# Chunk 2's last output half a step later, the first-used half of v loaded first, one load of q moved, and the packing of an output reversed

## The chip, the cores and the metric

The kernel runs on one core of a Trainium2 chip. The metric is the device time of one execution in microseconds (us), median of several runs. A profile of one further execution shows when each engine worked: TensorE (PE for matmuls, PEld for the loads of their weights), VectorE (DVE), ScalarE (ACT), GpSimd (POOL) and SyncE (SP). SP, ACT and POOL each have a queue from which they issue transfers (DMA); sixteen DMA engines, shared by these queues, carry them out.

## What is computed

A gated recurrence over 768 tokens for 4 batches and 8 heads of 48 channels, followed by a gated MLP over all 3072 tokens:

```python
f = 1.0 / (1.0 + np.exp(-f_logit))                 # q, k, v, f_logit: (4, 8, 768, 48)
for t in range(S):
    state = f[:, :, t, :, None] * state + np.einsum('bhd,bhe->bhde', k[:, :, t], v[:, :, t])
    y[:, :, t] = np.einsum('bhd,bhde->bhe', q[:, :, t], state)
x = y.transpose(0, 2, 1, 3).reshape(B * S, H * D)  # (3072, 384)
g = x @ w_gate                                     # (384, 1536)
out = (g / (1.0 + np.exp(-g)) * (x @ w_val)) @ w_out
```

## The kernel before

**Units and chunks.** The tokens are cut into six chunks of 128, c = 0 to 5. One chunk of one batch is a unit (b, c); its number is u = 4c + b (`units`, L397). The recurrence of a unit (`attention`, L630) is a generator of fifteen steps: load and transpose f, k and q, running products of f, scores (L754), masks, the output y (L826 from the state, L837 from the chunk itself), the new state (dS, L808) and the packing of y into xT (`copy_y`, L841). In chunk 3, say, these run while TensorE works on the MLP of chunk 2: TensorE's own stream is the MLP, and the recurrence of the next chunk is put into it piece by piece.

**The MLP of a chunk** (`mlp_fifteen`, L1097, for chunks 1 to 5) first forms sums of its tokens on VectorE (`token_sums`, L1105), then runs four blocks of fifteen products (L1143, into the PSUM banks A, B, o and c) and then the way down (`down_seven`, L1223): seven products `one` to `seven` of 24 matmuls each (L1246, L1309), each in two half steps of twelve. xT has three rows of 128 features (row 0, 1, 2) for 512 tokens. The first of the token sums, t14, needs rows 1 and 2 for batches 0 and 1. The second, t15, needs row 2 for all batches, and the fourth (on 512 columns) needs all three rows for batches 2 and 3. The last product `seven` leaves its results (`ob`) to two VectorE sums that stand behind the token sums of the next chunk. One of their inputs, u5, lies in the room `c22`, which ScalarE's copy of the second product (`c<-B`, L1148) overwrites at the start of the next chunk; the fifth product goes into bank B and waits for that copy.

**The order.** Tables of times say where in the MLP's stream each step of a unit stands: `SCORES` (when the scores come), `CHAINS` (the steps before them) and, in `times` (L1012), the time of each output. They are in microseconds of a model of TensorE's stream; `down[n]` is the n-th half step of the way down. `in_turn_of_time` (L1317) writes the instructions down in that order, and `in_order` (L896) keeps each engine's instructions in it. The last output of each chunk 2 to 5, that of batch 3, stands at `down[9]`: before the second half of `four` (o5, whose second half works on the hidden sums `hs`).

**Loads.** From unit 5 on, f, k and q are loaded in four pieces of 96 KB each into one room per name (`load`, L486). As there is one room, the next unit's load is issued right behind the step that emptied the room: `load_after(u, "f")`, `load_after(u, "k")` and `load_after(u, "q")` (L675, L687 or L721, L734). kT is turned by way of DRAM: four transfers out (L718) and one back as `kt` (L771 or L779), which dS reads.

**The two halves of v.** The score matrix of a unit is cut in blocks of 64 keys. L837 needs v in its usual place and, for the blocks that lie in the other half of the partitions, a second copy of parts of v, which `load_other_v` (L453) brings in two transfers of 48 KB: n = 0 for heads 0 to 3, n = 1 for heads 4 to 7. L837's loop takes the first 64 keys of all heads first. There the heads with `a` = 2 or 3 (heads 4 to 7) read the second copy; heads 0 to 3 read it in the second round.

**Packing.** `copy_y` copies y to SBUF with two ScalarE copies (even heads, then odd heads) and moves it into xT by ten transfers (L852), a head at a time, 48 features each, cut where a row of xT ends. GpSimd issues them, apart from units of chunks 0 and 1 with b < 3, where SP does.

**Completion semaphores.** The transfers of the queues of SP and ACT share eight completion semaphores and take them in turn. A transfer whose semaphore still belongs to one in flight waits on its queue for that one to land. GpSimd's transfers share another eight.

Of the kernel before, what the change touches and what calls it, by code (L numbers as in the profile page):

```python
# [290 lines left out]
def short_path(ctx, tc, ident, least, judge, q, k, v, f_logit, moe_w_gate, moe_w_val, moe_w_out, out):  # L291
# [10 lines left out]
    B, H, S, D = q.shape  # L302
# [13 lines left out]
    SQUARES = 2  # L316
# [80 lines left out]
    units = [(b, c) for c in range(NCH) for b in range(B)]  # L397
# [35 lines left out]
    def in_halves(u):  # L433

        b, c = units[u]
        return c > 0

    def blocks_of_keys(t, top, a, keys):

        t = t[top * CH:(top + 1) * CH]
        if keys:
            return t[:, (2 + a % 2) * CH:(3 + a % 2) * CH]
        return t.rearrange("p (two c) -> p two c", two=2)[:, :, a % 2 * CH:(a % 2 + 1) * CH]

    def other_v(A):

        return A.rearrange("p r a t -> p (r a t)")[:, 12 * CH:].rearrange("p (h e) -> p h e", e=W)

    def load_other_v(A, u):  # L453
        b, c = units[u]
        for n in range(2):
            since = c * C + (1 - n) * CH
            queue = nc.gpsimd if c < SQUARES and b == B - 1 else nc.sync
            queue.dma_start(out=other_v(A)[n * CH:(n + 1) * CH, :, 0:D],
                            in_=v[b, n * HP:(n + 1) * HP, since:since + CH, :].rearrange("h t d -> t h d"))
# [10 lines left out]
    def split_squares(nm):  # L470
        return squares(nm).rearrange("t a (j i) e -> t a j i e", j=2)
# [5 lines left out]
    def parted(t):  # L477

        return t.rearrange("p (j a t i) -> p a j i t", j=2, a=HP, i=NI // 2)
# [4 lines left out]
    def load(u, what="fkqv"):  # L486
        b, c = units[u]
        rows = slice(c * C, (c + 1) * C)
        inputs = dict(f=f_logit, k=k, q=q, v=v)
        for nm in "fqkv" if c >= SQUARES else "fvkq" if by_squares(u) else "fkqv":  # L490
            src = inputs[nm]
            if nm not in what:
                continue
            if nm == "v":
                dst = v_of(u)
            elif not by_squares(u):
                dst = raw[nm][u % NRAW]
            else:
                since = len(traced)
                for n in range(4):  # L500
                    at = Q * (1 - n % 2)
                    (nc.sync if c >= SQUARES else nc.gpsimd).dma_start(
                        out=rooms[nm][Q * n:Q * (n + 1), at:at + HP * RUN].rearrange("t (a e) -> t a e", a=HP),
                        in_=src[b, n // 2::2, rows, :].rearrange("a (t i) d -> t a (i d)", i=NI))
                if c < SQUARES:
                    by_pool.extend(ins for ins in traced[since:] if ins.engine == mybir.EngineType.Pool)
                    keep_order(by_pool[-5:])
                continue
            queue = nc.gpsimd if nm == "v" and c < SQUARES and (by_squares(u) or u in (1, 2)) else nc.sync
            for heads in (slice(0, HP), slice(HP, H)) if u == 0 and nm == "f" else (slice(0, H),):  # L510
                queue.dma_start(out=dst[:, heads, 0:D], in_=src[b, heads, rows, :].rearrange("h t d -> t h d"))
# [118 lines left out]
    def attention(u):  # L630
        b, c = units[u]
# [51 lines left out]
        if in_squares:  # L683
            kp = qT.rearrange("p a t -> p (a t)")
            nc.vector.transpose(parted(kp), split_squares("k"))
            if not turned or u == SQUARES * B:
                load_after(u, "k")  # L687
        yield

        n = HP * N1  # L690
        owner["tail", rot] = owner["start"] = u
        owned(u, ("gate", rot))
        for part in parts:
            at = slice(part.start * N1, part.stop * N1)
# [36 lines left out]
        if in_squares:  # L731
            qp = tail[:, 0:HP * C]
            nc.vector.transpose(parted(qp), split_squares("q"))
            load_after(u, "qv" if c < SQUARES else "q")  # L734
        yield
        owned(u, ("gate", rot), ("tail", rot))
        if halves and c < SQUARES:
# [74 lines left out]
        if halves:  # L812

            y = [bank("y") for _ in range(2)]

            def place(a, par, part=slice(0, W)):
                return y[a // 2][W * (a % 2) + part.start:W * (a % 2) + part.stop, par * C:(par + 1) * C]  # L820

            def of_state(pars_of, parts, first):
                for part in parts:
                    for a in range(HP):
                        par = pars_of(a)
                        nc.tensor.matmul(place(a, par, part), lhsT=decayed[rows_of(par), a, part], rhs=qT[rows_of(par), a, :],  # L826
                                         start=first, stop=False, skip_group_check=True)

            of_state(lambda a: 1 - a // 2, [slice(0, Q), slice(Q, W)], True)
            if SQUARES <= c < NCH - 1:  # L830
                dS = new_state()
            of_state(lambda a: a // 2, [slice(0, W)], False)
            for keys in range(2):
                for par in range(2):
                    for a in (0, 2, 1, 3):
                        h, top = 2 * a + par, a // 2
                        nc.tensor.matmul(queries_of_keys(place(a, par, slice(0, W if keys == top else D)), keys), rhs=blocks_of_keys(flat[par], top, a, keys),  # L837
                                         lhsT=(v_[:, h, :] if keys == top else other_v(A)[:, h % HP, 0:D])[top * CH:(top + 1) * CH],
                                         start=False, stop=keys == 1, skip_group_check=True)

            def copy_y():  # L841
                yT = att.tile([128, 2, TB // 2], FP32, tag="x", name="yT")
                for par in range(2):
                    nc.scalar.copy(yT[:, par, :], y[par][:, 0:HP // 2 * C])  # L844
                for h in range(H):
                    a, par = h // 2, h % 2
                    f = h * D
                    while f < (h + 1) * D:
                        n = min((h + 1) * D, (f // 128 + 1) * 128) - f
                        r = W * (a % 2) + f - h * D  # L850
                        queue = nc.sync if c < SQUARES and b < B - 1 else nc.gpsimd
                        queue.dma_start(out=xT[c][f % 128:f % 128 + n, f // 128, b * C:(b + 1) * C],  # L852
                                        in_=yT[r:r + n, a // 2, par * C:(par + 1) * C])
                        f += n

        else:


            y = bank("y")
            met = set()  # L860

            def add(n, lhsT, rhs, last):
                nc.tensor.matmul(y[Q * (n % 4):Q * (n % 4) + Q, n // 4 * C:(n // 4 + 1) * C], lhsT=lhsT, rhs=rhs,
                                 start=n % 4 not in met, stop=last, skip_group_check=True)
                met.add(n % 4)

            per = 2 * D // Q
            flat = v_.rearrange("t h e -> t (h e)")
            for par in range(2):
                for n in range(DM // Q):  # L870
                    h = n // per * 2 + par
                    at = n * Q - h * D
                    if -Q < at < D:
                        add(n, flat[:, W * h + at:W * h + at + Q], A[:, par, h // 2, :], par == 1 or at + Q <= D)
            nc.scalar.copy(xT[c][:, :, b * C:(b + 1) * C], y[:, 0:DM].rearrange("p (a t) -> p a t", t=C))
# [3 lines left out]
        if halves:  # L879
            copy_y()  # L880
# [10 lines left out]
    def load_after(u, what):  # L891

        if u + 1 < len(units) and u + 1 != SQUARES * B:
            load(u + 1, what)
# [99 lines left out]
    def chain(k, q, qmul, turn=None, head=None):  # L994
# [5 lines left out]
    down = [NJ * TRIPLE + n * DOWN / 2 - 0.05 for n in range(14)]  # L1000
# [5 lines left out]
        (chain(2.6, 4.8, 8.6), chain(14.5, 21.7, 23.2, 21.2, 19.6), chain(30, 37, 43.6), chain(57.4, 56.6, 61)),  # L1006
        (chain(-12, -8.5, -5), chain(3.5, 6, 9), chain(16, 28, 33, 21.5, 23.5), chain(40.1, 53, 55, 44.5, 52)),
        *[(chain(-21.4, -13.2, -11.5), (-7.5, -6.3, 1.3, 2.2, 3.2, 5.5, 8, 10), chain(16, 28, 33, 21.5, 23.5), chain(40.1, 53, 55, 44.5, 52))] * (NCH - 4)))}
    LAST = down[9]
    APART = {1: (1, 3), 2: (1, 2), **{c: (2,) for c in range(3, NCH - 1)}, NCH - 1: range(1, NJ)}  # L1010

    def times(c):  # L1012
        at = [t for t, _ in SCORES[c]]
        outputs = [*at[1:], down[9] if c + 1 in SCORES and SCORES[c + 1][0][0] < -1 else LAST]
        sigmoid = [-14 if c == 3 else SCORES[c - 1][-1][0] - whole - 0.01 if c > 3 else 0, -1.5 if c == 3 else at[0] - 0.01, *[t - 0.01 for t in at[1:]]]
        masks = {"b": 2, "o": 0.9, "A": 1.5}
        return [[f, *steps, s + 0.02, s + masks[kind], s + 2.2, o, o + 0.01, o + 2.1]
                for f, steps, (s, kind), o in zip(sigmoid, CHAINS[c], SCORES[c], outputs)]
# [504 lines left out]
```

## Time and profile before

| | us |
|---|---|
| median of 3 runs | 593.06 (592.43 to 593.49) |
| profiled execution | 589.34 |
| its span, first to last instruction | 587.6 |
| chunk 1's products begin | 136.5 |
| chunk 2's products begin | 231.95 |
| chunk 3's products begin | 323.67 |
| chunk 4's products begin | 415.98 |

The granted TensorE clock is 1.00 throughout. Lines of the profile read so: start (or line), duration, engine, source line, operation, what is written <- what is read, shape, number of instructions merged in the row, and in brackets the idle time of the engine before it and what ended it. In the chain of work that ended last, each line has a start, a length and what the program was waiting for or doing. In the view of waits a line says which engine waited at which line for whom: total us, times, longest. Transfers that are issued by SP or ACT stand on their queues, SPq and ACTq. A span of several issues merged in one row runs from the first to the end of the last.

### The profile page before, as it was taken

Reading aid. Unit: us, or ns where it says so; the run is one execution under the profiler, and the core shown is the slowest. Engines: PE = TensorE matmul, PEld = TensorE weight load, DVE = VectorE, ACT = ScalarE, POOL = GpSimd, SP = SyncE. Lnnn points to the kernel's source line nnn. Section 1 sums busy time; section 2 is a strip of 40 time slices with the busy share of each in tenths; the row PEclk is TensorE's granted clock in tenths of the full one; section 3 lists DMA queues with packets and bytes.
Section 4 is the critical chain, followed back from the end, with each engine's and each line's share of the span. In section 5 each row is a group of like instructions: output and inputs, shape, how many; then the busy total and the mean of one; then the engine's idle time right before and its main releaser. Section 6 shows DMA issues by size and latency. Waiting matters only on the chain.

```text
span 587.6 us, 12443 instructions
## 1 busy us (share of the span) xinstructions
PE 573.3 (98%) x4641; PEld 472.9 (80%) x4641; DVE 468.5 (80%) x825; ACT 303.7 (52%) x589; POOL 144.1 (25%) x307
## 2 busy tenths in 40 slices
PE   7999999999999989999999999999999999999996
PEld 4744445567888978888999788899988899988996
DVE  8888998999989975998985978986878971766641
ACT  2587778006887412666740476732376820356600
POOL 5140444341142334031233030333030323000000
PEclk9999999999999999999999999999999999999999
DMA  9999696434669557453446433434341100100001
GB/s 180 279 283 285 190 249 147 88 103 131 130 151 144 117 126 180 125 107 79 101 108 153 114 89 73 104 93 120 112 115 28 35 17 16 58 2 2 0 1 57
DMA packets 122643, 65.97 MB, mean 112 GB/s; under 512 B 79616, under 2 KB 112992, under 8 KB 122576
## 3 DMA queue, kind: packets, MB, share of 16 engines
q1 hardware_dynamic: 108508, 48.62, 33.7%
q0 software_dynamic: 12784, 14.67, 10.9%
q10 hardware_dynamic: 1284, 1.84, 0.9%
q8 instruction: 37, 0.61, 0.4%
q14 instruction: 30, 0.25, 0.1%
HBM read 50.14 MB, written 8.65 MB: 100 GB/s over the span
## 4 chain that ended last, share of the span: by engine, by line
PE 85%; DMA 6%; DVE 3%; ACT 2%; issue 2%; SPq 1%; ACTq 0%; POOL 0%; DVEq 0%
PE A L1143 17%; PE o L1246 15%; PE B L1143 14%; PE c L1143 6%; PE o L950 5%; PE gate L927 5%; PE val L927 5%; PE o L1143 5%; PE o L1309 3%; DMA kt<-turn 2%; PE y L826 2%; PE y L837 2%; PE sc L754 2%; PE dS L808 2%; DMA fraw<-in_f_logit_dram 2%
## 5 line engine op out<-in xcount | busy, mean ns | idle before, releaser
L852 POOL DMA_DIRECT2D xT<-yT x170 | 84.8, 508 | 91.6 <-ACT yT L844 83.2
L1143 PE MATMUL A<-xs,w_both 128*128 128x256 f32 x240 | 61.8, 380 | 0.0
L1246 PE MATMUL o<-w_out,h 128*128 128x192 f32 x360 | 61.2, 326 | 0.0
L1246 PEld LDWEIGHTS o<-w_out,h 128*128 128x128 f32 x360 | 59.0, 190 | 0.4
L1148 ACT COPY aside<-A 128x512 f32<-128x512 f32 x60 | 35.1, 585 | 33.1 <-PE A L1143 33.1
L1148 ACT COPY c<-A 128x512 f32<-128x512 f32 x40 | 23.3, 583 | 54.9 <-PE A L1143 44.5
L1044 DVE TENSOR_TENSOR c<-c,aside 128x512 f32<-128x512 f32 x60 | 41.2, 686 | 12.6 <-ACT aside L1148 10.6
L1143 PEld LDWEIGHTS A<-xs,w_both 128*128 128x128 f32 x240 | 45.2, 190 | 6.3
L1095 DVE TENSOR_TENSOR h<-h,c 128x256 f32<-128x256 f32 x100 | 40.4, 412 | 6.1 <-ACT h L1159 5.7
L741 POOL MEMSET gates<- 128x4 f32 x24 | 3.7, 153 | 161.4 <-DVE qT L648 155.5
L1047 DVE TENSOR_TENSOR c<-c,aside 128x512 f32<-128x512 f32 x60 | 40.9, 682 | 2.6 <-ACT aside L1148 2.6
L844 ACT COPY yT<-y 128x256 f32<-128x256 f32 x40 | 12.8, 370 | 58.6 <-PE y L837 42.0
L1143 PE MATMUL B<-xT,extra 128*128 128x256 f32 x160 | 41.3, 380 | 0.9 <-ACT c L1148 0.9
L1246 PE MATMUL o<-ws,h 128*128 128x192 f32 x240 | 41.7, 328 | 0.0
L1159 ACT ACTIVATE h<-c 128x256 f32<-128x256 f32 x100 | 39.2, 416 | 4.8 <-DVE c L1044 3.5
L1143 PE MATMUL A<-xs,extra 128*128 128x256 f32 x160 | 41.3, 380 | 0.3 <-ACT c L1148 0.2
L1143 PE MATMUL B<-xs,w_both 128*128 128x256 f32 x160 | 41.3, 380 | 0.0
L1143 PE MATMUL c<-xT,w_both 128*128 128x256 f32 x160 | 41.1, 379 | 0.0
L1148 ACT COPY aside<-B 128x512 f32<-128x512 f32 x60 | 35.1, 585 | 9.6 <-PE B L1143 7.3
L1246 PEld LDWEIGHTS o<-ws,h 128*128 128x128 f32 x240 | 39.3, 190 | 0.5
L1047 DVE TENSOR_TENSOR c<-o,c 128x512 f32<-128x512 f32 x40 | 27.3, 683 | 10.0 <-ACT h L1159 5.8
L1143 PEld LDWEIGHTS B<-xT,extra 128*128 128x128 f32 x160 | 30.2, 190 | 5.7 <-ACT c L1148 1.6
(173 smaller groups left out, 1250.0 us busy)
## 6 DMA issues: line engine op xcount, KB each, us to landing
fsquares<-in_f_logit_dram SPq DMA_DIRECT2D x64, 96.0 KB, 2.8
qsquares<-in_q_dram SPq DMA_DIRECT2D x64, 96.0 KB, 2.5
ksquares<-in_k_dram SPq DMA_DIRECT2D x64, 96.0 KB, 2.4
w<-in_moe_w_gate_dram SPq DMA_DIRECT2D x6, 768.0 KB, 8.1
w<-in_moe_w_val_dram SPq DMA_DIRECT2D x6, 768.0 KB
w<-in_moe_w_out_dram SPq DMA_DIRECT2D x6, 768.0 KB, 4.7
v<-in_v_dram SPq DMA_DIRECT2D x19, 192.0 KB, 5.3
kt<-turn SPq DMA_DIRECT2D x11, 256.0 KB
```

The lines of the kernel that those rows point to most:

```text
L844: nc.scalar.copy(yT[:, par, :], y[par][:, 0:HP // 2 * C])
L852: queue.dma_start(out=xT[c][f % 128:f % 128 + n, f // 128, b * C:(b + 1) * C], in_=yT[r:r + n, a // 2, par * C:(par + 1) * C])
L927: nc.tensor.matmul(p, lhsT=w[:, j, i, :], rhs=xT[c][:, i, :], start=(i == 0), stop=(i == KT - 1))
L950: nc.tensor.matmul(p, lhsT=hidden_tile(h, n // 2)[:, n % 2 * 2 + b // 2, b % 2 * C:(b % 2 + 1) * C], rhs=w_out[:, j, :], start=(n == 0), s ...
L1044: nc.vector.tensor_tensor(dst, a, b, ALU.add)
L1047: nc.vector.tensor_tensor(dst, a, b, ALU.subtract)
L1095: lagging.append(lambda: f(*args))
L1143: nc.tensor.matmul(p[name][:, n, :], lhsT=weights_of[a][:, n, j, :], rhs=tokens[b], start=fresh and n == 0, stop=True, skip_group_check=True)
L1148: nc.scalar.copy(t, p[name])
L1159: nc.scalar.activation(dst, src[:, 0, :], AF.Silu)
L1246: nc.tensor.matmul(p[:, n, :], lhsT=lhsTs[j][:, n * C:(n + 1) * C], rhs=rhs[:, j, :], start=first and j == order[0] and n == 0, stop=j == ...
L1309: nc.tensor.matmul(p, lhsT=hidden_tile(h, j)[:, 2, n * C:(n + 1) * C], rhs=b22[:, j, :], start=j == order[0], stop=j == order[-1])
```

## The change

Four edits. The last output of chunk 2 is set to `down[10]`, behind the second half of `four`; those of later chunks stay at `down[9]`. `load_other_v` issues n = 1 before n = 0, for all units that use it. For the units b = 1 of chunks 4 and 5 (`behind`), the load of q is no longer issued behind the step that emptied its room (the transposition of q of unit (0, c)) but behind the unit's own transposition of k. `copy_y` sends the pieces of xT from head 7 to head 0.

```diff
+    def behind(u):
+
+        return u < len(units) and units[u][1] > SQUARES + 1 and units[u][0] == 1
...
     def load_other_v(A, u):
         b, c = units[u]
-        for n in range(2):
+        for n in (1, 0):
...
             kp = qT.rearrange("p a t -> p (a t)")
             nc.vector.transpose(parted(kp), split_squares("k"))
+            if behind(u):
+                load(u, "q")
             if not turned or u == SQUARES * B:
                 load_after(u, "k")
...
             qp = tail[:, 0:HP * C]
             nc.vector.transpose(parted(qp), split_squares("q"))
-            load_after(u, "qv" if c < SQUARES else "q")
+            if not behind(u + 1):
+                load_after(u, "qv" if c < SQUARES else "q")
...
-                for h in range(H):
+                for h in reversed(range(H)):
                     a, par = h // 2, h % 2
...
-    LAST = down[9]
...
-        outputs = [*at[1:], down[9] if c + 1 in SCORES and SCORES[c + 1][0][0] < -1 else LAST]
+        outputs = [*at[1:], down[9] if c > SQUARES else down[10]]
```

(`SQUARES` is 2; before, both branches of `outputs` gave `down[9]`.) On TensorE, this is chunk 2's last output (unit 11; y, dS) before the change, with the first half of `four` (on hs_1375) ahead of it. Line numbers are those of the kernel before.

```order
L1246 MATMUL o_2184<-ws_1370,hs_1375 128x192 x6
L826 MATMUL y<-qT,decayed 32x128 x8
L808 MATMUL dS<-v_127,kt 64x48 x8
L826 MATMUL y<-qT,decayed 64x128 x4
L837 MATMUL y<-A,v_127 64x128
L837 MATMUL y<-A 48x128
```

The same place after it; the code below the edits has moved down by six or seven lines, so that L826, L808 and L837 are now L833, L815 and L844.

```order
L1252 MATMUL o_2184<-ws_1370,hs_1375 128x192 x6
L1252 MATMUL o_2184<-ws_1370,hs_1376 128x192 x6
L833 MATMUL y<-qT,decayed 32x128 x8
L815 MATMUL dS<-v_127,kt 64x48 x8
L833 MATMUL y<-qT,decayed 64x128 x4
L844 MATMUL y<-A,v_127 64x128
```

The row on hs_1376, second half of `four`, now stands ahead of y instead of behind it; nothing else on TensorE moves. On SP's queue, this is the end of chunk 3 before the change: unit (0, 4) has been turned, the loads of k and q for unit (1, 4) follow, then kt and the second copy of v for unit (0, 4), and loads for later units.

```order
L718 DMA turn<-ksquares 512x1x32 x4
L502 DMA ksquares<-in_k_dram 32x4x192 x4
L502 DMA qsquares<-in_q_dram 32x4x192 x4
L771 DMA kt<-turn 128x1x512
L458 DMA A<-in_v_dram 64x4x48 x2
L511 DMA v_127<-in_v_dram 128x8x48
L502 DMA fsquares<-in_f_logit_dram 32x4x192 x4
```

After it:

```order
L724 DMA turn<-ksquares 512x1x32 x4
L506 DMA ksquares<-in_k_dram 32x4x192 x4
L778 DMA kt<-turn 128x1x512
L462 DMA A<-in_v_dram 64x4x48 x2
L515 DMA v_127<-in_v_dram 128x8x48
L506 DMA fsquares<-in_f_logit_dram 32x4x192 x4
L506 DMA qsquares<-in_q_dram 32x4x192 x4
```

The four loads of q have moved behind kt, v and f. At the end of chunk 4 the same happens: q's loads move from behind kt and v of chunk 4's last unit to behind f, and now stand ahead of the next loads of k. On GpSimd's queue the ten pieces of an output stood in this order, here those of chunk 2's last output:

```order
L852 DMA xT<-yT 48x128 x2
L852 DMA xT<-yT 32x128
L852 DMA xT<-yT 16x128
L852 DMA xT<-yT 48x128 x2
L852 DMA xT<-yT 16x128
L852 DMA xT<-yT 32x128
L852 DMA xT<-yT 48x128 x2
```

They now stand in this one:

```order
L859 DMA xT<-yT 48x128 x2
L859 DMA xT<-yT 16x128
L859 DMA xT<-yT 32x128
L859 DMA xT<-yT 48x128 x2
L859 DMA xT<-yT 32x128
L859 DMA xT<-yT 16x128
L859 DMA xT<-yT 48x128 x2
```

The first two pieces are now heads 7 and 6, and the piece of 32 features that follows is the last of row 2. Two more things move in the opening part, where the order is not written out: one load of v (`v_127`, L511) comes ahead of ten pieces of xT on SP's queue, and VectorE's second and third token sums of chunk 1 come ahead of a few sums of weights.

## The prediction, before the changed kernel was run

> **What bounds the kernel now.** The page comes first: which engine is full.
>
> ```profile
> PE 573.3 (98%) x4641; PEld 472.9 (80%) x4641; DVE 468.5 (80%) x825; ACT 303.7 (52%) x589; POOL 144.1 (25%) x307
> ```
>
> TensorE is the bound. No matmul is added or removed, so only TensorE's waits can move the time. The view of waits says for what it stands still longest:
>
> ```profile
> PE y L837 <- DMA A<-in_v_dram: 1.9, 1, 1.9
> ```
>
> Shorter waits, for kt's landing and for ScalarE, are shown below. I price each by the distance between starts, since modelled ends hide a part.
>
> **Term 1: chunk 2's last output.** TensorE's timeline there, and then the same step in chunk 3, where nothing is late:
>
> ```profile
> 211.18 4.06 PE L1246 MATMUL o<-ws,h 128*128 128x192 f32 x24
> 215.08 2.11 PE L1246 MATMUL o<-ws,hs 128*128 128x192 f32 x12
> 217.12 0.45 PE L826 MATMUL y<-qT,decayed 48*32 48x128 f32 x16
> 218.18 0.67 PE L808 MATMUL dS<-v,kt 128*64 128x48 f32 x16 [0.61 <-DMA kt<-turn]
> ...
> 221.29 0.31 PE L837 MATMUL y<-A 64*48 64x128 f32 x1 [1.86 <-DMA A<-in_v_dram]
> ...
> 222.10 2.22 PE L1246 MATMUL o<-ws,hs 128*128 128x192 f32 x12
> ...
> 231.95 1.03 PE L1143 MATMUL A<-xs,w_both 128*128 128x256 f32 x4
> ...
> 233.74 1.13 PE L1143 MATMUL B<-xs,w_both 128*128 128x256 f32 x4
> ```
>
> ```profile
> 311.11 0.45 PE L826 MATMUL y<-qT,decayed 48*32 48x128 f32 x16
> 311.49 0.67 PE L808 MATMUL dS<-v,kt 128*64 128x48 f32 x16
> ...
> 312.36 0.28 PE L837 MATMUL y<-A,v 64*64 64x128 f32 x2
> ...
> 312.70 0.32 PE L837 MATMUL y<-A 64*48 64x128 f32 x4
> ...
> 313.02 0.86 PE L754 MATMUL sc<-qT,kT 48*64 48x128 f32 x32
> ```
>
> Undisturbed, an output takes 313.02 - 311.11 = 1.91 us; here it takes 222.10 - 217.12 = 4.98, so 3.07 us are waiting. What it waits for stands in the chain, in SP's timeline and waits, and in the view of transfers:
>
> ```profile
> 211.36 6.78 DMA kt<-turn
> ...
> 218.15 3.09 DMA A<-in_v_dram
> ```
>
> ```profile
> 213.91 4.87 SPq L458 DMA_DIRECT2D A<-in_v_dram  x2
> ```
>
> ```profile
> SPq L458 <- DMA kt<-turn: 3.6, 1, 3.6
> ```
>
> ```profile
> A<-in_v_dram SPq DMA_DIRECT2D x2, 48.0 KB, 6.1
> ```
>
> The first half of the other v is issued at 213.91 and lands 6.1 us later, at 220.0. The second waits on SP until kt has landed (218.14), because it uses the completion semaphore that kt used, and lands at 221.24. The half read first (heads 4 to 7) is now the second one. Nothing that delays these transfers depends on TensorE's place, so I leave their times as they are.
>
> The change puts twelve matmuls (o5 on hs) ahead of this output. Twenty-four take 215.08 - 211.18 = 3.90 us, so twelve take 1.95. The output then starts at 219.07; kt has landed, and the 0.68 us lost there is gone. L837 starts 312.36 - 311.11 = 1.25 later, at 220.32, when the first-read half is in SBUF (220.0). The other half is wanted 312.70 - 312.36 = 0.34 later, at 220.66, and is there at 221.29: a wait of 0.6 us that no part of the change removes. After 0.32 us more the output ends at 221.61. Before, the same work was done at 222.10 + 1.95 = 224.05. **Gain: 2.4 us.**
>
> What is late next is the hand-over to chunk 2's products, which TensorE now reaches at 231.95 - 2.44 = 229.5. GpSimd's timeline there, the landing of these pieces, and VectorE's timeline:
>
> ```profile
> 222.91 4.98 POOL L852 DMA_DIRECT2D xT<-yT  x10 [8.86 <-ACT yT L844]
> ```
>
> ```profile
> DMA to landing us min/median/max: 1.9/2.4/2.8
> ```
>
> ```profile
> 231.10 0.68 DVE L1044 TENSOR_TENSOR xs<-xT 128x512 f32<-128x512 f32 x1
> ...
> 233.96 0.61 DVE L1044 TENSOR_TENSOR ob<-c,o 128x192 f32<-128x192 f32 x2
> ```
>
> The last of the ten pieces of xT is issued 0.5 us before 227.89 and lands near 230.1. The output now ends 0.49 earlier, but the first piece (head 7) needs the second yT copy, estimated at 0.3 us later, so all pieces are there at 229.9. From the sum of 512 columns (231.10), which reads all three rows of xT, to the last ob sum is 233.96 + 0.61 - 231.10 = 3.47 us; it would end at 233.5. ScalarE's copy c<-B overwrites the room that ob reads (0.6 us, next section), so the fifth product can start at 234.2. It would be due at 229.5 + 3.44 (chunk 3: 326.25 - 323.67 for three products, and one more of 0.86) + 0.93 for the scores between (233.74 - 231.95 - 0.86) = 233.9. **Given back: 0.3 us. Term 1: 2.1 us.** The ends: 3.07 if every wait goes; -0.8 if the last piece takes as long as the slowest landing of the next section (5.56 us instead of the 2.7 from 227.2 to 229.9).
>
> [...] The rows have 1.9 to 2.8 us here, up to 5.56 below, so the sum goes by the rows.
>
> **Term 2: packing from the last head, and q behind it (start of chunk 3's products).** The chain, then VectorE's, ScalarE's and TensorE's timelines:
>
> ```profile
> 314.46 5.56 DMA xT<-yT
> ...
> 320.30 2.79 DMA xT<-yT
> ```
>
> ```profile
> 323.21 0.43 DVE L1050 SCALAR_TENSOR_TENSOR xs<-xT 128x256 f32<-128x256 f32 x1 [1.30 <-DMA xT<-yT]
> ```
>
> ```profile
> 327.57 0.58 ACT L1148 COPY c<-B 128x512 f32<-128x512 f32 x1 [2.26 <-DVE ob L1044]
> ```
>
> ```profile
> 323.67 1.03 PE L1143 MATMUL A<-xs,w_both 128*128 128x256 f32 x4
> ...
> 326.25 1.03 PE L1143 MATMUL A<-xs,w_both 128*128 128x256 f32 x4
> 328.21 1.13 PE L1143 MATMUL B<-xT,extra 128*128 128x256 f32 x4 [0.93 <-ACT c L1148]
> ```
>
> The chain is long: a piece of xT lands after 5.56 us, the tenth is issued only then and lands at 323.08; VectorE's second sum, which needs only row 2 of xT, waits 1.30 us for it; every later sum, the ob sums, ScalarE's copy and the fifth product slide with it. That product starts 328.21 - 326.25 = 1.96 after the fourth instead of 0.86: 1.10 us lost.
>
> Reversed packing sends row 2 in the first four pieces. Alone it lets the two sums on row 2 (0.4 us each) run before the last piece lands, and only the 512-column sum wait for it: 0.8 us. Four loads of q (96 KB each, 1.86 us of SP's queue) go in front of these pieces now:
>
> ```profile
> 311.95 1.86 SPq L502 DMA_DIRECT2D qsquares<-in_q_dram  x4
> ...
> 318.36 6.04 SPq L502 DMA_DIRECT2D fsquares<-in_f_logit_dram  x4
> ```
>
> ```profile
> 333.64 0.71 DVE L733 STREAM_TRANSPOSE tails<-qsquares 128x512 f32<-128x512 f32 x1
> ```
>
> Behind f they leave the pieces to themselves until 318. If the landing shrinks by 0.7 us, which the 2.4 of the section before allows easily, the wait is gone. **Term 2: 1.1 us** (ends 0.8 and 1.1; zero if f and q now collide with the last pieces). q is issued by 324.4 + 1.9 = 326.3 and read at 333.64, so even a landing of 6.3 us is in time; past that VectorE's queue would stop behind that transpose.
>
> [...] The 5.56 us beside 2.4 show that something shares; not that it is q.
>
> **Term 3: chunk 4's last output.** The chain, SP's and TensorE's timelines:
>
> ```profile
> 397.79 5.97 DMA kt<-turn
> ```
>
> ```profile
> 401.18 1.74 SPq L502 DMA_DIRECT2D qsquares<-in_q_dram  x4
> ```
>
> ```profile
> 402.99 0.45 PE L826 MATMUL y<-qT,decayed 48*32 48x128 f32 x16
> 403.81 0.67 PE L808 MATMUL dS<-v,kt 128*64 128x48 f32 x16 [0.36 <-DMA kt<-turn]
> ```
>
> dS starts 0.82 after the output instead of 0.38: 0.44 lost to kt. kt's issue does not move; only q's loads leave the last third of its flight. Between 0 and 0.44 I take **0.2 us**.
>
> **At nothing:** the other outputs, whose halves of v are not waited for now, and v's load in the opening, which moves ahead of ten pieces of xT on SP (1.37 us of its queue):
>
> ```profile
> 101.09 1.37 SPq L511 DMA_DIRECT2D v<-in_v_dram  x1
> ```
>
> ```profile
> 125.26 0.42 DVE L1047 TENSOR_TENSOR xs<-xT 128x256 f32<-128x256 f32 x1
> ```
>
> Their reader comes 24 us later; without that cover it would cost the 1.37.
>
> **The sum.** 2.1 + 1.1 + 0.2 = 3.4 us. The profiled execution would go from 589.34 to 585.9; the median of the runs, 3.72 us above it, from 593.06 to 589.7. Waits are absolute times, so I carry the difference over unscaled.
>
> **The rivals.**
> 1. *The move of q buys nothing*: terms 2 and 3 shrink to 0.8 and 0: a gain of 2.9, 590.2 us. For it: q's last loads may have landed before the slowest piece. Against: the slow landings stand only where SP has just issued loads.
> 2. *The wait moves to the hand-over*: chunk 2's xT pieces take 4.5 us instead of 2.7, because out stores and loads of the next unit now follow closer. 1.8 us go back: 591.5 us. At 5.56 us, 2.9 go back and 592.6 us is left, no change.
> 3. *Slower*: the same place, if the last piece lands 8 us after its issue. The fifth product then waits 5.6 us instead of 0.3, the sum is -1.9 and the time 595.0. It decides from a landing of 2.7 + 3.4 = 6.1 us on; the slowest rows (6.1 for half of v) lie where kt shares the engines, and kt is done at 218.14.
> 4. *The half step does nothing*, because the halves land later too: SP's row shows no wait for TensorE there, so I give it little; 591.8 us.
>
> **How the numbers follow.** Forecast 0.57, rival 1 0.17, rival 2 0.14 (a third of it without change), rival 3 0.04, rival 4 0.04, and 0.04 for slides of queues that I don't see. What a measurement can tell from no change is about 0.2%, 1.2 us. Faster 0.84, within 0.12, slower 0.04. The range runs from 588.5, where all waits go (3.07 + 1.1 + 0.44), to 591.7, which holds rival 1 and the milder half of rival 2.
>
> **What would show it.** Right: dS of chunk 2's last output starts 0.38 after it; L837 waits about 0.6 us, at its second half; the ob sums end before ScalarE wants c<-B at chunk 3's start; xT's pieces land there within 3 us. Wrong: a fifth product of chunk 2 that waits over 1 us, xT still landing after 5 us, or a VectorE stop ahead of the transposition of q.

## The result, and the profile after

The median fell from 592.74 us (591.90 to 593.49, 4 runs) to **586.07 us** (585.55 to 586.44, 4 runs): a ratio of 0.9887, 95% interval 0.9870 to 0.9904. The direction and the places were right, the size was not: 6.67 us were gained where 3.4 were forecast, and 586.07 lies below the range. The profiled executions, however, lie only 3.0 us apart: 589.34 before, 586.33 after. The changed kernel's profile is like its timed runs; the earlier kernel's profile was 2.6 us quicker than the quickest of its timed runs.

The page of the changed kernel, engines first. TensorE is as full as before:

```profile
PE 575.0 (98%) x4641; PEld 474.3 (81%) x4641; DVE 468.2 (80%) x825; ACT 303.6 (52%) x589; POOL 144.4 (25%) x307
```

TensorE's timeline at chunk 2's last output and at the start of its products (L833, L815 and L844 are the former L826, L808 and L837):

```profile
215.69 4.06 PE L1252 MATMUL o<-ws,hs 128*128 128x192 f32 x24
219.69 0.45 PE L833 MATMUL y<-qT,decayed 48*32 48x128 f32 x16
220.07 0.67 PE L815 MATMUL dS<-v,kt 128*64 128x48 f32 x16
...
221.08 0.31 PE L844 MATMUL y<-A 64*48 64x128 f32 x1
...
221.89 4.17 PE L1252 MATMUL o<-w_out,h 128*128 128x192 f32 x24
...
229.80 1.03 PE L1149 MATMUL A<-xs,w_both 128*128 128x256 f32 x4
...
233.41 1.03 PE L1149 MATMUL A<-xs,w_both 128*128 128x256 f32 x4
234.66 1.13 PE L1149 MATMUL B<-xT,extra 128*128 128x256 f32 x4 [0.22 <-ACT c L1154]
```

All 24 matmuls of `four` now stand ahead. dS starts 0.38 us after the output (1.06 before): kt isn't waited for. The output takes 221.89 - 219.69 = 2.20 us (4.98 before, 1.91 undisturbed). The fifth product follows the fourth by 1.25 us instead of 0.86, so 0.39 us are given back. Chunk 3's products and chunk 4's last output, in the same view:

```profile
324.59 1.03 PE L1149 MATMUL A<-xs,w_both 128*128 128x256 f32 x4
325.45 1.03 PE L1149 MATMUL B<-xT,extra 128*128 128x256 f32 x4
```

```profile
400.13 0.45 PE L833 MATMUL y<-qT,decayed 48*32 48x128 f32 x16
400.51 0.67 PE L815 MATMUL dS<-v,kt 128*64 128x48 f32 x16
```

Here the fifth product follows at 0.86 and dS at 0.38: both waits are gone. So far the trace does what the prediction said. What it doesn't show is why the kernel before, when timed, is some 3 us slower than its profile. The whole change run a second time, further down, gained 5.2 us with an interval of 3.1 to 6.3, so the size of the gain itself is known to a microsecond or two only.

### The profile page after: what moved, and what is told of

It is laid out like the page before. It is cut to its first block, busy times and chain, and to the rows that moved or that the text cites. A ratio compares the mean times of both kernels' runs of the same rounds, so it can differ in the third digit from the quotient of the medians.

```text
span 584.5 us, 12432 instructions
## 1 busy us (share of the span) xinstructions
PE 575.0 (98%) x4641; PEld 474.3 (81%) x4641; DVE 468.2 (80%) x825; ACT 303.6 (52%) x589; POOL 144.4 (25%) x307
## 4 chain that ended last, share of the span: by engine, by line
PE 83%; DVE 8%; ACT 3%; DMA 3%; issue 2%; POOL 1%; SPq 0%; DVEq 0%; ACTq 0%; POOLq 0%
PE o L1252 20%; PE A L1149 17%; PE B L1149 14%; PE c L1149 6%; PE o L1149 5%; PE o L1315 3%; PE o L957 2%; PE gate L934 2%; PE y L833 2%; PE y L844 2%; PE sc L761 2%; PE dS L815 2%; PE val L934 2%; DMA kt<-turn 1%; PE sc L766 1%
## 5 line engine op out<-in xcount | busy, mean ns | idle before, releaser
L1149 PEld LDWEIGHTS A<-xs,extra 128*128 128x128 f32 x160 | 30.2, 190 | 5.1 <-ACT c L1154 1.1
```

The source lines that it names most:

```text
L1149: nc.tensor.matmul(p[name][:, n, :], lhsT=weights_of[a][:, n, j, :], rhs=tokens[b], start=fresh and n == 0, stop=True, skip_group_check=True)
```

## The experiments

### The kernel before once more

No edit. 

> The kernel before, unchanged, profiled a second time. Theory A (the profiled execution of before was a lucky one; an ordinary execution of it waits some 3 us longer, and the change removes those waits too): this execution takes 592 to 593.5 us, and its trace shows about 3 us more than the first one between the same milestones (first products of chunks 1 to 5: intervals of 95.64, 91.72, 92.31 and 87.61 us, the end 79.38 after the last of them), at places that the change touches: the landing of kt and of the halves of v at the last outputs of chunks 2 and 4, and of xT at the hand-overs. Rival B (the executions of before differ somewhere that the change doesn't touch, and the changed kernel is faster there by something else): the same 592 to 593.5 us, but the extra time lies in the opening or in other stretches. Rival C (profiled executions of before are always 3 us faster than timed ones): 589.3 us again, with the same intervals to 0.3 us.

Ten executions took 589.24 to 592.63 us, median 591.33; 29 of the same kernel beside them 589.77 to 595.30, median 592.15. The profiled one took 590.99, under the 592 to 593.5 that theories A and B had. Its busy time by stretches of 1 us (length, busy time of PE, PEld, DVE, ACT and POOL with counts, the granted TensorE clock, the DMA share and GB/s):

```profile
220.00:221.00 1.00, 0.00 (x0) 0.00 (x0) 0.00 (x0) 0.00 (x0) 0.00 (x0) 1.00 0.94 180
221.00:222.00 1.00, 0.80 (x23) 0.80 (x25) 0.00 (x0) 0.00 (x0) 0.00 (x0) 0.74 0.66 177
222.00:223.00 1.00, 1.00 (x19) 0.87 (x12) 0.00 (x0) 0.39 (x2) 0.00 (x0) 0.50 0.76 208
223.00:224.00 1.00, 1.00 (x5) 1.00 (x4) 0.61 (x1) 0.48 (x3) 0.73 (x2) 0.50 0.50 92
224.00:225.00 1.00, 1.00 (x5) 1.00 (x4) 0.10 (x1) 0.98 (x2) 1.00 (x3) 0.56 0.72 121
225.00:226.00 1.00, 1.00 (x8) 1.00 (x7) 0.10 (x1) 0.99 (x2) 1.00 (x3) 1.00 0.80 141
```

**The granted clock falls to 0.50 right after the wait**, and TensorE does five matmuls in a microsecond where it does eight later. The stretch of 220 to 225 us in the first profile, and the same in this one:

```profile
220.00:225.00 5.00, 3.71 (x48) 3.65 (x49) 1.36 (x3) 1.69 (x5) 2.09 (x5) 1.00 0.74 157
```

```profile
220.00:225.00 5.00, 3.80 (x38) 3.67 (x39) 0.71 (x1) 1.85 (x5) 1.73 (x4) 0.66 0.72 156
```

TensorE's timeline of this profile shows the wait and its price:

```profile
217.31 0.45 PE L826 MATMUL y<-qT,decayed 48*32 48x128 f32 x16
218.00 0.67 PE L808 MATMUL dS<-v,kt 128*64 128x48 f32 x16 [0.24 <-DMA kt<-turn]
...
221.20 0.31 PE L837 MATMUL y<-A 64*48 64x128 f32 x1 [1.95 <-DMA A<-in_v_dram]
...
222.46 3.39 PE L1246 MATMUL o<-ws,hs 128*128 128x192 f32 x12
225.69 4.06 PE L1246 MATMUL o<-w_out,h 128*128 128x192 f32 x24
...
233.49 1.03 PE L1143 MATMUL A<-xs,w_both 128*128 128x256 f32 x4
```

Together the waits are no longer than in the first profile (0.24 for kt instead of 0.61, 1.95 for the half of v instead of 1.86). But the twelve matmuls behind them take 225.69 - 222.46 = 3.23 us. In the first profile the row behind that of 222.10 is this one, so it was 224.15 - 222.10 = 2.05 there:

```profile
224.15 4.06 PE L1246 MATMUL o<-w_out,h 128*128 128x192 f32 x24
```

From chunk 1's first product to chunk 2's it is 97.13 us instead of 95.64, and the later intervals are the same to 0.04.

Theory A, longer waits, falls; B and C fall too. A **clock theory** takes their place: the idle time makes the granted clock fall to half for some microseconds afterwards, in most executions of the kernel before, though not in the one that the prediction read.

### Parts of the change alone

Only the half step:

```diff
-        outputs = [*at[1:], down[9] if c + 1 in SCORES and SCORES[c + 1][0][0] < -1 else LAST]
+        outputs = [*at[1:], down[9] if c > SQUARES else down[10]]
```

> Only chunk 2's last output half a step later; v's halves, q and the packing as before. Theory A: kt's 0.68 us goes and most of the wait for the two halves; the half read first (heads 4 to 7) is still the second one and lands at 221.24, where it is wanted at 220.32, so 0.9 us of waiting stay instead of 0.6, and 0.3 us are given back at the hand-over: 1.8 us of gain by the waits of the first profiled execution, and 3 to 5 if ordinary executions of before wait longer there: 588 to 591 us against a before of 592.7. Rival B (the extra gain comes from another part, the order of SP's loads above all): 591 us.

Measured: 586.77 us (585.92 to 588.53), ratio 0.9911, interval 0.9889 to 0.9933: 5.4 us gained, and the time lies below the 588 to 591 us that I had written. The profiled execution is the slowest of the six (588.53); its chunks 1 and 2 together take 185.56 us all the same, against 188.84 in before_again. Its clock is 1.00 up to 580 us, and the mean clock of all six is 0.998 to 1.00. In the whole change, too, the stretch that the wait stood in is full and the clock stays up:

```profile
220.00:225.00 5.00, 5.00 (x87) 4.81 (x76) 2.26 (x5) 0.65 (x2) 2.02 (x5) 1.00 0.68 156
```

Part of half_alone's gain is given back at chunk 2's products, more than in the whole change:

```profile
233.31 1.03 PE L1143 MATMUL A<-xs,w_both 128*128 128x256 f32 x4
235.11 1.13 PE L1143 MATMUL B<-xT,extra 128*128 128x256 f32 x4 [0.77 <-ACT c L1148]
```

1.80 us instead of 0.86, so 0.94 lost at chunk 2's products.

Only the order of the halves (`for n in (1, 0):` for `for n in range(2):`):

> Only the half of v that is read first is loaded first; the step of the output is as before. Theory A: the first half lands at 220.0 where L837 wants it at 219.4, the second at 221.24 where it is wanted 0.34 later: the wait of 1.86 us is split and its end stays, so the output ends where it did: a gain of 0 to 0.3 us, 592.5 us against 592.7. Rival B: 0.5 us or more, if the order of the halves changes how they land.

Measured: 592.18 us (589.34 to 593.68), ratio 0.9995 (0.9974 to 1.0016): no gain, as expected. In its trace the wait is split, 1.12 and 0.33 us, and the clock is low for twice as long:

```profile
220.00:225.00 5.00, 3.85 (x37) 3.34 (x38) 0.71 (x1) 1.01 (x4) 1.58 (x4) 0.62 0.66 146
225.00:230.00 5.00, 5.00 (x23) 5.00 (x23) 1.42 (x3) 1.84 (x3) 3.50 (x8) 0.70 0.79 186
```

Only the packing from the last head on (`for h in reversed(range(H)):`):

> Only the packing from the last head on; SP's loads of q stay ahead of the packing, and one load of v in the opening moves ahead of ten pieces of xT on SP's queue, as it does in the whole change. By the prediction: 0.8 us of the 1.10 lost at the start of chunk 3's products go: 591.9 us against 592.7. Rival B (the extra gain of the whole change comes with the order of the loads in the opening): 589.5 us, and the interval between the first products of chunks 1 and 2 falls from 95.64 by 2 us or more. Rival D (the last pieces of xT land late whichever row they hold, and the sum of 512 columns now waits where the sum of 256 did): no change to 0.2 us.

Measured: 590.87 us (588.87 to 592.16), ratio 0.9980 (0.9964 to 0.9996): 1.3 us gained. The interval of chunk 1 is 97.84 us, so rival B falls. The fifth product of chunk 3 follows the fourth at 1.36 us:

```profile
328.78 1.03 PE L1143 MATMUL A<-xs,w_both 128*128 128x256 f32 x4
330.14 1.13 PE L1143 MATMUL B<-xT,extra 128*128 128x256 f32 x4 [0.34 <-ACT c L1148]
```

That is 0.60 us less than in the first profile of before (1.96) and 0.83 less than in the second (2.19).

### The idle time filled

Now the clock theory is put to the test. If the idle time lowers the clock, then work put into the idle time should keep it up, though the waits stay.

```diff
             of_state(lambda a: a // 2, [slice(0, W)], False)
+            for n in range(14 if u == 11 else 0):
+                nc.tensor.matmul(place(2, n % 2), lhsT=causal[CH:C, 0:W], rhs=causal[CH:C, :],
+                                 start=False, stop=False, skip_group_check=True)
```

(`causal[64:128, 0:64]` is zero, so y doesn't change.)

> The kernel before, with 14 matmuls of zeros (64x64 by 64x128, added to y, about 0.11 us each, 1.5 us in all) in chunk 2's last output, ahead of the first product that reads a late half of v: TensorE does them in a wait that the kernel before spends idle. The waits for kt and for the halves stay. Clock theory (the granted clock halves for one or more stretches of 3.41 us after this idle time, 1.7 us lost in each, and that is the part of the gain which no wait explains): the clock stays at 1.00 at 221 to 228 us, the time falls to 589.3 to 589.8 us against 592.2, and the spread from 6 us to about 1. Rival (ordinary executions lose the time in longer waits): no change, 592.2, or up to 1.5 us slower where the fillers outlast the wait.

The control has `u == 15`, chunk 3's last output:

> The same 14 matmuls in the last output of chunk 3 instead, where TensorE waits for nothing. Clock theory: they are work on the path and remove no idle time, so the stall of chunk 2 and its clock stay: 592.2 + 1.5 = 593.7 us. If this one gets faster too, the fillers act by something other than the idle time that they fill.

Two more have 7 and 3 in place of 14 at unit 11:

> As filled, with 7 matmuls of zeros instead of 14. The 14 took 3.0 us (28 records of about 0.107 us) and outlasted the wait by 0.9; 7 take 1.5 us and fit into the 1.9 to 2.1 us of it. Clock theory: no window of 3.41 us at 217 to 222 us holds under 2.25 us of work, the clock stays at 1.00 in nearly all executions, and the time is that of the executions of before at a clock of 0.998 or more: 589.0 to 589.7 us, some 2.3 us under before, with 1.5 us of work added. Rival (the waits grow): 591.3 to 592.2.

> [...] In the traces so far the clock halved after windows of 1.25 to 2.05 us and stayed after one of 2.25. Clock theory: it falls in some executions and not in others: clocks on both sides of 0.998, a median of 590 to 591.5. Rival: no change from before.

Measured, in us. An execution counts as having kept its clock when the mean over its span is 0.998 or more. That is strict: the clock also falls around the end, to a mean of 0.93 over 580.0 to 584.5 us in the changed kernel's profile, where no matmul runs, and filled_half's profiled execution, at 1.00 up to 580 us and 0.77 over 580 to 590, has a mean of 0.997 from this alone.

| kernel | median of all | before beside it | ratio, interval | clock kept | median where kept |
|---|---|---|---|---|---|
| filled | 590.83 | 591.28 | 1.0006 (0.9981 to 1.0031) | 10 of 12 | 590.68 |
| filled_elsewhere | 593.64 | 591.28 | 1.0038 (1.0021 to 1.0055) | 0 of 12 | |
| filled_half | 591.27 | 591.81 | 1.0001 (0.9978 to 1.0023) | 6 of 12 | 590.51 |
| filled_a_little | 589.14 | 591.81 | 0.9979 (0.9953 to 1.0005) | 7 of 12 | 588.69 |

The times miss what I wrote. None of the three is shown to be quicker than before, and the forecast spread of 1 us isn't there. One reason is plain in filled's trace: each of the 14 matmuls is two records of 0.107 us, so they take 3.0 us, not 1.5, and outlast the wait by some 0.9. That explains only a part: the executions of filled that kept their clock took 590.68 us, 1.4 more than those of before that did (589.24).

```profile
218.90 2.89 PE L834 MATMUL y<-causal 64*64 64x128 f32 x25
```

What holds is the contrast. The same 14 matmuls cost 2.4 us at unit 15, and in the trace there chunk 2's interval grows by 3.05 us (94.76 against 91.71); at unit 11 they cost nothing measurable. And the clock: it was kept in 23 of 36 executions with fillers in the idle time, in none of 12 with fillers elsewhere, and in 9 of 91 executions of the kernel before. On one chip alone, beside each other, it was 10 of 12 for filled, none of 12 for filled_elsewhere and 4 of 29 for before. Within one kernel the time goes with the clock: filled_a_little took 588.69 us (median) in the seven executions that kept it and 592.78 in the five others. The two stretches behind the wait, filled and then filled_elsewhere:

```profile
220.00:225.00 5.00, 5.00 (x66) 4.93 (x65) 0.74 (x2) 1.70 (x5) 1.46 (x3) 1.00 0.70 152
225.00:230.00 5.00, 5.00 (x33) 5.00 (x32) 2.49 (x6) 1.16 (x2) 3.65 (x9) 1.00 0.90 205
```

```profile
220.00:225.00 5.00, 3.58 (x37) 3.45 (x38) 0.83 (x2) 1.57 (x5) 1.30 (x3) 0.57 0.68 148
225.00:230.00 5.00, 5.00 (x25) 5.00 (x24) 1.42 (x3) 1.29 (x2) 3.79 (x9) 0.75 0.90 206
```

Half the fillers kept the clock in half the executions, fewer than I expected, and three matmuls did so about as often as seven, so the share doesn't grow evenly with the work put in. That the work in some 3.41 us decides, with a limit near 2.25 us, was my assumption for these two; no run shows it. Why the executions of filled_half that kept it took 589.95 to 592.38 us, over 1 us more than those of before that did, is open: its profiled one (590.07, clock 1.00 up to 580 us) shows only 0.42 us more in chunk 1.

### The whole change without one part

Without the half step:

```diff
-        outputs = [*at[1:], down[9] if c > SQUARES else down[10]]
+        outputs = [*at[1:], down[9] if c + 1 in SCORES and SCORES[c + 1][0][0] < -1 else LAST]
```

> The whole change but for the half step: half of v read first loaded first, reversed packing, q behind it. Clock theory: the wait at chunk 2's last output stays (kt 0.2 to 1.0, halves of v 1.5 to 2.1 us), so the clock still halves in most executions; terms 2 and 3 give 1.1 and 0.4: 590.7 us against 592.2, the spread still 4 us or more. Rival (the 3 us come with the order of SP's loads): 587 to 588 us and a narrow spread.

Measured: 589.51 us (587.39 to 591.17), ratio 0.9975 (0.9960 to 0.9989): 1.8 us gained, not 5 or 6. The clock was kept in one execution of twelve, and that is the quickest, 587.39. The waits stand where they stood (0.72 us for kt, 0.81 and 0.42 for the halves), and so does their price:

```profile
220.00:225.00 5.00, 4.16 (x40) 3.80 (x41) 0.71 (x1) 1.51 (x5) 1.78 (x4) 0.66 0.69 152
```

Chunk 3's interval is 90.69 us, the same as in the whole change.

Without the move of q (`behind` and both of its uses left out):

> The whole change but for q: its loads stay ahead of the packing. By the prediction term 2 shrinks from 1.1 to 0.8 and term 3 to nothing: 0.5 us slower than the whole change, 586.6 us. If q's move buys nothing at all: 586.1. If it carries term 2 (the pieces of xT land late because four loads of q stand ahead of them): the fifth product of chunk 3 still waits 0.5 us or more, dS of chunk 4's last output 0.2 to 0.4, and 587.2 us.

Measured: 586.36 us (585.29 to 587.70), ratio 0.9920 (0.9897 to 0.9943). The medians can't part 0.3 us; the trace can:

```profile
324.31 1.03 PE L1143 MATMUL A<-xs,w_both 128*128 128x256 f32 x4
325.77 1.13 PE L1143 MATMUL B<-xT,extra 128*128 128x256 f32 x4 [0.43 <-ACT c L1148]
```

The distance is 1.46 us instead of 0.86, and chunk 3's interval 91.39 instead of 90.69: the 0.7 us belong to the move of q. The chain of this kernel has xT's second piece landing after 6.05 us:

```profile
312.79 6.05 DMA xT<-yT
...
319.12 2.32 DMA xT<-yT
```

With q behind the packing the same piece took 3.73 us in the whole change, and 4.14 and 3.56 in the next two kernels.

Without the reversal (`for h in range(H):`), and the whole change again:

> The whole change but for the reversed packing. At the start of chunk 3's products the pieces of xT, with no q ahead of them, land some 3 us after their issue and nothing waits: interval from chunk 3's first product to chunk 4's 90.7 us as in the whole change. At the start of chunk 2's products row 2 of xT comes last again: the fifth product waits 0.8 us instead of 0.2, as with the half step alone, and the interval of chunk 2 is 92.75 instead of 92.2. Together 0.5 us slower than the whole change: 586.5 us. If the reversal also carries the start of chunk 3: 1 us or more slower.

> The whole change, unchanged, on the same chip as these: 586.0 us, executions within 1.5 us of each other, the clock at 0.999 or 1.00 in each of them; before at 0.993 to 0.996 in most. If executions of it fall to 0.996 as well, the clock isn't what parts the two kernels.

Measured on one chip: 585.77 us (585.68 to 586.50), ratio 0.9909 (0.9884 to 0.9933), and 586.58 us (585.20 to 588.21), ratio 0.9921 (0.9894 to 0.9948). The reversal isn't worth a measurable time once q stands behind the packing. In the trace of the kernel without it the fifth product follows at 1.60 us in chunk 2 and at 1.04 in chunk 3; in whole_again at 0.93 and 0.89. The intervals of chunks 2 and 3 sum to 183.52 and 182.70 us, so 0.8 us of waiting, which the medians don't confirm. One of the six executions of the whole change had a clock of 0.995 (588.03 us). So a fall may still come, rarely; where, isn't known, as that execution left no trace. Two others took 587.31 and 588.21 us with the clock up; why, isn't known either. The six lie 3.0 us apart, twice what I had written.

## Why the prediction was right in its places and wrong in its size

**Where the 6.67 us are.** The timed executions of before in the first comparison have no clock on record, so the split comes from later ones. These are all executions of the two kernels with a clock on record, but for the first profile of before (589.34, clock 1.00), by their mean clock:

| mean granted clock | kernel before: executions, median us | whole change: executions, median us |
|---|---|---|
| 0.998 or more | 9, 589.24 | 9, 585.85 |
| 0.995 to 0.997 | 34, 591.36 | 1, 588.03 |
| 0.994 or less | 48, 592.36 | none |

Among executions with the clock up, the kernels lie 589.24 - 585.85 = 3.39 us apart. That is the part that waits explain, and the forecast was 3.4; that the two agree so closely is partly luck, as either group spreads over 2 to 3 us and the terms missed one by one (below). The rest goes with the clock: 82 of 91 executions of before lose 2 to 3 us more (as medians), and the change, with 0.3 us of waiting left at that place, nearly always escapes it. Against the median of those that fell furthest, 592.36, that is 592.36 - 589.24 = 3.1 us. The clock alone is enough for such losses: the three groups' mean clocks average 0.9988, 0.9958 and 0.9932, which over 590 us is 1.8 and 3.3 us less of full speed than in the first group (an estimate), against 2.1 and 3.1 measured. Longer waits aren't it: in the six traces with a fall, TensorE's waits at this output come to 1.9 to 3.1 us, and in the first profile, without a fall, to 2.5. On each of the three chips the groups lie 2.2 to 2.5 and 3.2 to 3.4 us apart. The clock follows the half step: it was kept in 26 of 27 executions of kernels that have it, and in 11 of 139 of kernels that have neither it nor fillers at unit 11.

**The step that failed** is the last of the sum: "Waits are absolute times, so I carry the difference over unscaled." The profiled execution (589.34, clock 1.00) was one of the tenth that keep the clock, and I took its cost of an idle microsecond, one microsecond, for the ordinary one. In an ordinary execution the granted clock falls to half at this output, during its last wait or within 0.5 us of it, for 3.41 or 6.83 us in the six traces that have it, and the waiting, 3.07 us in term 1, goes with another 2 to 3 us. The warning was on the page: the profile was 3.1 us quicker than the quickest of three timed runs, which lay within 1.1 us of each other. I wrote the 3.72 us down as an offset of the median instead of asking what the timed runs have that the profile lacks. The upper end of the gain, "all waits go", had the same hole, so the range was cut off at 588.5.

Point by point:

- **Term 1, forecast 2.1, was 2.4 us** (chunks 1 and 2 together 187.35 us before, 184.91 after). kt's wait went, as written. The remaining wait in the output was 0.3 us, not 0.6, and stood at the first late half, since that half landed at 221.04 and not at 220.0. Given back: 0.39 us (0.07 in whole_again), forecast 0.3. The ends of this term priced every wait at full clock.
- **Term 2, forecast 1.1, was 1.10 us** (1.96 to 0.86). Of the parts, the reversal alone gives 0.6 to 0.8 (forecast 0.8), the move of q alone 0.9 (1.96 to 1.04, in the kernel without the reversal); they overlap. By the place of q the rows read: 5.3 to 6.6 us for the second piece in eight of the ten traces with q ahead of it, 3.6 to 4.1 in the four with q behind. But what held the piece back, q's own bytes or something else, isn't shown. On SP's queue q also stood ahead of kt (256 KB): before, kt was issued at 313.90, as the first piece was (313.96); in the whole change it was issued at 310.54, 2 us ahead of that piece (312.57). No run moves the one without the other.
- **Term 3, forecast 0.2, was 0.44 us** in the pair of profiles (dS 0.82 after the output before, 0.38 after). In the ten traces without the move of q the wait varied from 0 to 0.6 us, with one of 1.1, so 0.2 is a fair guess; in the four with it there was none.
- **At nothing:** right. Chunk 1's first product came at 137.08 us instead of 136.31 (the 136.5 in the table above is the chain's figure, where the other starts are the timeline's), but among kernels whose opening is that of before it varied from 135.87 to 137.26. In the pair of profiles this later start, 0.8 us, hides part of the gain: terms 1 to 3 come to 2.4 + 1.1 + 0.4 = 3.9 us, and 3.0 are left.
- **Rivals.** 1 falls (the move of q carries 0.7 us in the traces of without_q and after, though their medians can't show it); 2 and 3 fall, as the pieces of xT landed 1.9 to 2.7 us after their issue at chunk 2's hand-over; 4 falls, as the half step alone gained 5.4 us. None of them had the clock in it.

## What to carry to other kernels

Here waits of TensorE cost more than their length: those at one output, 1.9 to 3.1 us in the six traces with a fall, went with another 2 to 3 us (as medians) in 82 of 91 executions of the kernel before. So look at the granted clock in the stretches behind a wait, and in more than one execution, since the fall came in some and not in others. If a profile is quicker than every timed run, first ask which cost it lacks, before a difference is carried from the one to the other. If a late transfer can't be brought forward, the work behind it can be moved ahead of it: here one half step of matmuls gained 5.4 us alone, most of what the whole change did.

## What the runs showed of the hardware that was not expected

**In all six traces with a fall, the clock is low for 3.41 us or twice that.** In before_again it fell to 0.50 near 221.5 us and was back at 224.9; in halves_alone it was low from 221.2 to 228.0, twice as long. The edges, in stretches of 0.1 us of the two kernels:

```profile
221.40:221.50 0.10, 0.10 (x11) 0.10 (x8) 0.00 (x0) 0.00 (x0) 0.00 (x0) 0.85 0.80 231
...
224.80:224.90 0.10, 0.10 (x2) 0.10 (x2) 0.00 (x0) 0.10 (x1) 0.10 (x1) 0.58 0.81 118
```

```profile
221.10:221.20 0.10, 0.10 (x12) 0.10 (x5) 0.00 (x0) 0.00 (x0) 0.00 (x0) 0.93 1.28 238
...
228.00:228.10 0.10, 0.10 (x2) 0.10 (x1) 0.10 (x1) 0.00 (x0) 0.10 (x1) 0.94 1.01 284
```

The 33 rows of 0.1 us between these two of before_again all read 0.50, those outside 1.00. If the clock has one of these two values within a row too, the row's mean tells when it changed: 0.85 puts the fall at 221.47 and 0.58 the return at 224.88, 3.41 us later. In the second kernel it is 221.19 to 228.01, 6.83 us with less rounding. Worked out in the same way, three more traces give 3.41 us and one 6.83. 3.41 us at half clock are 1.7 us of full speed less (an estimate: half of the 3.41). Once or twice that roughly fits the groups of the table above (2.1 and 3.1 us).

**TensorE was not idle in the 3.41 us ahead of a fall.** These are the 3.41 us before the fall in before_again, and a later stretch of the same length in the same kernel, at the waiting fifth product of chunk 3, after which the clock stayed:

```profile
218.07:221.48 3.41, 1.46 (x36) 1.16 (x40) 1.75 (x2) 0.00 (x0) 0.00 (x0) 1.00 0.49 100
...
327.29:330.70 3.41, 2.25 (x11) 1.67 (x10) 3.34 (x9) 1.07 (x2) 1.11 (x2) 1.00 0.09 34
```

In the six traces with a fall, the 3.41 us before it held 1.25 to 2.05 us of matmuls; the second row here has 2.25. No single wait of TensorE at these falls was longer than 2.14 us. That the 3.41 us before a fall are the ones that count, and where the second row begins, is my choice; no run shows it, and none gives a limit. Nor do the traces show why much the same wait stands beside a halved clock in one execution, before_again (1.95 us for a half of v), and not in another, the first profile of before (1.86).
